# The queries of a windowed-attention kernel kept in the column order of their transposes

## The chip, the cores and the metric

The kernel runs on one core of a Trainium2 chip. The metric is the device time of one launch in microseconds. TensorE does matmuls and transposes, VectorE (DVE) and ScalarE (ACT) element-wise work, GpSimd (POOL) casts and small copies, and SyncE (SP) issues nearly all DMAs. SBUF is the on-chip memory, 128 partitions wide; matmuls write to PSUM.

## The reference

Attention over 4 batches, 8 heads, 768 positions of 64 numbers, and then a feed-forward layer over the 3072 tokens:

```
scores = scale * q @ k.T
keep   = is_global | is_local            # is_global: key < 8; is_local: 0 <= query - key < 96
bias   = -slopes[h] * dist               # dist: query - key, or 96 for a far global key
a      = softmax(where(keep, scores + bias, -1e9))
x      = (a @ v) as tokens x 512
out    = max(x @ w1, x @ w2, x @ w3) @ w_out     # 512 -> 768 -> 512
```

The inputs and the output are float32; the kernel's matmuls take bfloat16.

## The kernel before, in words

The tokens are cut into 24 tiles T of 128, six for each batch (NT = 6). A query tile needs its own keys and those of the tile before it (ds = 0, 1); the 8 global keys are copied over the first keys of each tile's transposed k. Scores are kept transposed, keys on the partitions and queries on the columns, so that exp(scores) can be the weights of the matmul with v. The bias is either multiplied in after the exponential (as exp(bias), VectorE, L319 and L321) or, for some tiles of batch 0, added ahead of it by a matmul with the identity (L289), for which the eight `bias` rows of L308 are made, one for each head.

All work is in one hand-written list, SCHEDULE (L25): each word is a unit, its tile and choices, and each engine meets its instructions in that order. Letters that matter here: `l` loads a pair of tiles of q or k (one part is 256 tokens; L148), `c` casts it (L180), `x` transposes it and copies the result to SBUF (`u_x`, L233), `S` makes the scores and the exponential of one tile and one half g of the heads (`u_S`, L282), `M` multiplies by the mask, `A` multiplies with v (L323), `T` transposes the result (L356), `F` and `O` are the two feed-forward matmuls (L376, L406), and `B` makes a bias row (`u_B`, L305), on ScalarE (0) or VectorE (1). The last number of `x` says which PSUM pool is used and which engine copies (odd: VectorE, even: ScalarE).

Tiles 0 to 11 (batches 0 and 1) come by `l`, `c`, `x`. Six q parts, and the last three k parts, are loaded with 8 neighbouring tokens on one partition (ET = 8, so that DMA descriptors are long): the row of partition (i, j) holds tokens 8i to 8i+7 of head j (and, by z, of head 4+j). So the eight transposes e = 0 to 7 (L255) give columns in the order (e, i, j), and the copy of L257 restores the order of the tokens for each head pair j: it reads PSUM with a step of 128 bf16 in its innermost run, and writes contiguous rows. The first three k parts have two neighbouring tokens on a partition and go by L250, one half copied by ScalarE and the other by VectorE. Tiles 12 to 23 come by other units (`L`, `C`, `X`), in token order.

In `u_S` one tile and one g have 8 score matmuls (4 for the first tile of a batch): weights are 64 rows by 128 keys, and the moving operand is 128 columns of q for the head pair jp. The halves z = 0 and 1 take partitions 0 to 63 and 64 to 127. They write `sp`, a PSUM tile of two banks with one buffer for each g; L302 is one exponential over all of it, 1024 columns (512 for the first tile of a batch), written as bfloat16 to `P`.

Of the kernel before, what the change touches and what calls it, by code (L numbers as in the profile page):

```python
# [14 lines left out]
AF = mybir.ActivationFunctionType  # L15
# [47 lines left out]
def kernel(  # L63
# [13 lines left out]
    nc = tc.nc  # L77
# [5 lines left out]
    NT = S // 128  # L83
    NTT = B * NT
    NP = H // 2
# [3 lines left out]
    scale = 1.0 / math.sqrt(D)  # L89
    slopes = [2.0 ** (-8.0 * (h + 1) / H) for h in range(H)]  # L90
    sizes = [4, 2, 2, 4, 4, 4, 4]

    ET = 8
# [30 lines left out]
    rbase = persist.tile([128, 3, 128], FP32, name="rbase")  # L124

    wmask = persist.tile([128, 2, 4, 3, 128], BF16, name="wmask")
    bias = persist.tile([128, 2, 2, 2, 3, 128], BF16, name="bias")
# [7 lines left out]
    raw, rawv, qb, qkT, Pt, xb = {}, {}, {}, {}, {}, {}  # L135
# [9 lines left out]
    def short_rows(n, s):  # L145
        return s == 1 and n < 3
# [31 lines left out]
    copies = (nc.scalar.copy, nc.vector.tensor_copy, nc.gpsimd.tensor_copy)  # L178
# [28 lines left out]
    def batch_T(b):  # L207
        if b not in qkT:
            qkT[b] = qkT_pool.tile([128, 2, NP, S], BF16, name="qkT", tag="qkT")
        return qkT[b]  # L210

    def qT(T, a):
        b, t = divmod(T, NT)
        return qkT[b][:, a, :, 128 * t:128 * t + 128]

    def put_kg(T, how):

        b, t = divmod(T, NT)
        kT = qT(T, 1)
        if t == 0:  # L220
            copies[how](kg8[b % 2], kT[:, :, 0:NG])
        elif t < NT - 1:
            copies[how](kT[:, :, 0:NG], kg8[b % 2])
# [9 lines left out]
    def u_x(n, s, how):  # L233
        b, t0 = divmod(2 * n, NT)
        dst = batch_T(b)[:, s, :, t0 * 128:(t0 + 2) * 128]
        if short_rows(n, s):
            dst = dst.rearrange("c j (i e) -> c j i e", e=2)
            if how == 4:
                halves = [(0, 2, psT, "tp", nc.scalar.copy), (2, 4, psH, "h", nc.vector.tensor_copy)]
            else:  # L240
                pool, tag = (psH, "h") if how in (2, 3) else (psT, "tp")
                halves = [(0, 4, pool, tag, copies[how % 2])]
            tps = [pool.tile([128, 2, hi - lo, 128], BF16, name="tpp", tag=tag) for lo, hi, pool, tag, copy in halves]
            for (lo, hi, pool, tag, copy), tp in zip(halves, tps):
                for e in range(2):
                    for j in range(lo, hi):
                        nc.tensor.transpose(tp[:, e, j - lo], qb["p", n, s][:, e, j].rearrange("p z d -> p (z d)"),
                                            identb)
            for (lo, hi, pool, tag, copy), tp in zip(halves, tps):
                copy(dst[:, lo:hi], tp.rearrange("c e j i -> c j i e"))  # L250
            return
        pool, tag = (psH, "h") if how in (2, 3) else (psT, "tp")
        tp = pool.tile([128, ET, 128 // NP, NP], BF16, name="tpp", tag=tag)
        for e in range(ET):
            nc.tensor.transpose(tp[:, e].rearrange("c i j -> c (i j)"),  # L255
                                qb["p", n, s][:, e].rearrange("p z d -> p (z d)"), identb)
        copies[how % 2](dst.rearrange("c j (i e) -> c j i e", e=ET), tp.rearrange("c e i j -> c j i e"))  # L257

    def u_X(T, how):
        pt = batch_T(T // NT)  # L260
# [21 lines left out]
    def u_S(T, g, how):  # L282
        b, t = divmod(T, NT)
        sp = psS.tile([128, 2, 2, 2, 128], FP32, name="sp", tag=f"sp{g}")
        n = 2 if t else 1
        if how:

            for hh in range(2):
                nc.tensor.matmul(sp[:, hh, :, 0:n], identb,  # L289
                                 bias[:, g, hh, :, 0:2] if t else bias[:, g, hh, :, 2:3],  # L290
                                 start=True, stop=False, skip_group_check=True)
        for ds in range(2 if t else 1):
            for i in range(2):
                jp = 2 * g + i
                for z in range(2):
                    hsl = slice(64 * z, 64 * z + 64)
                    nc.tensor.matmul(sp[:, z, i, ds], qT(T - ds, 1)[hsl, jp], qT(T, 0)[hsl, jp],  # L297
                                     start=not how, stop=True, skip_group_check=True)
        P = p_pool.tile([128, 4, 2, 128], BF16, name="P", tag="P")
        Pt[T, g] = P  # L300
        masked[T, g] = how
        nc.scalar.activation(P[:, :, 0:n], sp.rearrange("p a b d n -> p (a b) d n")[:, :, 0:n],  # L302
                             AF.Exp, bias=0.0, scale=scale)

    def u_B(h, how):  # L305
        z, g, i = h // 4, h % 4 // 2, h % 2
        mul = (nc.scalar.mul, nc.vector.tensor_scalar_mul, nc.gpsimd.tensor_scalar_mul)[how]
        mul(bias[:, g, z, i], rbase, -slopes[h] / scale)  # L308

    def u_K(h):  # L310
        z, g, i = h // 4, h % 4 // 2, h % 2
# [149 lines left out]
    with tc.manual_schedule():  # L461
        load_part(0, 0)
        load_part(0, 1)

        BIGD = 60000.0
        nc.gpsimd.iota(rbase[:, 0:2], base=0, pattern=[[128, 2], [1, 128]], channel_multiplier=-1,
                       allow_small_or_imprecise_dtypes=True)
        nc.vector.memset(tiny, 0.0)
        nc.scalar.activation(tiny, tiny, AF.Exp, bias=0.0, scale=1.0)
        nc.gpsimd.affine_select(rbase[:, 0:2], rbase[:, 0:2], base=(NL - 1),  # L470
                                pattern=[[-128, 2], [-1, 128]], channel_multiplier=1,
                                compare_op=ALU.is_ge, fill=BIGD)
        nc.vector.memset(zeros, 0.0)  # L473
        nc.gpsimd.affine_select(rbase[:, 0, :], rbase[:, 0, :], base=0,
                                pattern=[[1, 128]], channel_multiplier=-1,
                                compare_op=ALU.is_ge, fill=BIGD)
        nc.vector.memset(rbase[0:NG, 1, :], float(NL))
        nc.vector.tensor_copy(rbase[:, 2, :], rbase[:, 0, :])
        nc.vector.tensor_scalar_min(rbase[0:NG, 2, :], rbase[0:NG, 2, :], float(NL))
        make_identity(nc, identb)  # L480
        for tvar in va_ring + va_first:
            nc.vector.memset(heads(tvar)[:, :, 64:65], 1.0)

        units = {"l": load_part, "v": load_v, "c": cast_part, "x": u_x, "L": load, "w": load_w, "o": load_wo, "C": cast, "X": u_X, "S": u_S, "M": u_M,
                 "A": u_A, "G": put_kg, "V": put_vg, "T": u_XT, "F": u_F1, "W": cast_w,
                 "K": u_K, "B": u_B, "Q": cast_wo, "O": u_F2, "E": u_E, "D": u_D}
        for u in SCHEDULE.split():
            units[u[0]](*(int(n) for n in u[1:].split(".") if n))
# [33 lines left out]
```

## Time and profile before

| | us |
|---|---|
| median of 3 runs | 179.06 (178.82 to 180.25) |
| the profiled execution | 176.64 |
| its span, first to last instruction | 174.7 |
| TensorE busy | 168.3 (96%) |
| VectorE busy | 122.6 (70%) |
| ScalarE busy | 103.9 (59%) |
| GpSimd busy | 28.5 (16%) |
| granted TensorE clock | 1.000 |

The profile is a record of one execution. Its groups give, for each line, engine and shape, the count, the busy time and the mean duration, and then the engine's idle time ahead of these instructions with what ended it. The chain that ended last is followed back from the last instruction: at each step to what released it, or to the instruction before it on its engine. Matmuls are pipelined: one takes about 216 ns from start to end here, while the next starts much earlier, so their cost is read from groups that follow each other in the chain. TensorE's weight loads have their own row (PEld) and overlap with matmuls.

### The profile page before, as it was taken

How to read it: one execution, taken by the hardware profiler on the slowest of the kernel's cores; microseconds unless marked ns; L12 is line 12 of the kernel's file. 1: busy time of each engine (PE TensorE's matmuls, PEld its weight loads, DVE VectorE, ACT ScalarE, POOL GpSimd, SP SyncE). 2: the span in 40 equal slices, each digit the busy share in tenths (PEclk: the TensorE clock that was granted, in tenths of full speed). 3: DMA queues.
4: the chain of work that ended last, by engine and by line, in shares of the span. 5: the costliest groups of instructions: out<-in, count | busy, mean ns of one | idle time of the engine just before them, and what ended most of it. 6: DMA issues, size and time to landing. Idle time of an engine off the chain costs nothing.

```text
span 174.7 us, 3961 instructions
## 1 busy us (share of the span) xinstructions
PE 168.3 (96%) x1517; PEld 95.2 (54%) x1540; DVE 122.6 (70%) x254; ACT 103.9 (59%) x157; POOL 28.5 (16%) x58
## 2 busy tenths in 40 slices
PE   7879799999999999999999999999999999999996
PEld 2445555558866777854554454454544554444444
DVE  5478669897979799777888736799267993233720
ACT  7779769848999776776723665814857301342022
POOL 3245620100032521001041010203100300000000
DMA  4999999999999998999999899996965433401006
GB/s 134 323 283 284 327 341 342 383 387 385 239 228 211 283 248 160 158 264 236 196 188 231 119 298 254 204 195 120 249 158 155 89 94 90 180 0 60 6 3 237
DMA packets 82611, 36.44 MB, mean 209 GB/s; under 512 B 70048, under 2 KB 75040, under 8 KB 82592
## 3 DMA queue, kind: packets, MB, share of 16 engines
q1 hardware_dynamic: 82448, 36.12, 87.0%
q8 instruction: 12, 0.20, 0.5%
q10 hardware_dynamic: 144, 0.07, 0.1%
q14 instruction: 7, 0.06, 0.1%
HBM read 25.17 MB, written 6.29 MB: 180 GB/s over the span
## 4 chain that ended last, share of the span: by engine, by line
PE 90%; DMA 3%; SPq 2%; DVE 1%; issue 1%; ACT 1%; POOL 0%; DVEq 0%; POOLq 0%
PE h L382 54%; PE po L397 18%; PE sp L297 7%; DMA rawp<-in_q_dram 3%; PE op L336 3%; PE op L339 2%; PE tpp L255 2%; SPq L159 2%; PE oph L336 1%; PE wp L459 1%; PE sp L289 1%; PE xtp L370 1%; SPq L155 1%; ACT P L302 1%; DVE xT L371 1%
## 5 line engine op out<-in xcount | busy, mean ns | idle before, releaser
L382 PE MATMUL h<-xT,w 128*128 128x512 bf16 (+1 forms) x488 | 99.4, 348 | 1.1 <-issue 0.2
L382 PEld LDWEIGHTS <-w 128*128 128x128 bf16 x504 | 46.9, 98 | 40.0 <-issue 0.2
L302 ACT ACTIVATE P<-sp 128x1024 bf16<-128x1024 f32 (+1 forms) x48 | 43.6, 952 | 17.1 <-PE sp L297 16.9
L389 DVE TENSOR_TENSOR h<-h,h 128x512 bf16<-128x512 bf16 (+1 forms) x42 | 25.5, 608 | 15.9 <-PE h L382 13.0
L397 PE MATMUL po<-wo,ht 128*128 128x512 bf16 (+2 forms) x150 | 33.0, 362 | 0.3
L387 ACT CAST h<-h 128x512 bf16<-128x512 f32 (+1 forms) x42 | 21.8, 534 | 16.0 <-PE h L382 15.8
L391 DVE TENSOR_TENSOR ht<-h,h 128x512 bf16<-128x512 bf16 (+1 forms) x42 | 25.1, 606 | 4.5 <-PE h L382 3.2
L319 DVE TENSOR_TENSOR P<-P,wmask 128x1024 bf16<-128x1024 bf16 x35 | 24.5, 713 | 4.2 <-ACT P L302 4.2
L403 ACT COPY ost<-po 128x512 f32<-128x512 f32 (+2 forms) x17 | 9.4, 556 | 24.2 <-PE po L397 24.1
L397 PEld LDWEIGHTS <-ht 128*128 128x128 bf16 x156 | 14.3, 98 | 14.9
L297 PEld LDWEIGHTS <-qkT 64*128 64x128 bf16 x352 | 10.0, 94 | 10.0 <-issue 7.0
L297 PE MATMUL sp<-qkT 64*128 64x128 bf16 x352 | 14.7, 218 | 0.7 <-DVE qkT L257 0.3
L353 DVE TENSOR_TENSOR xb<-op,rz 128x512 bf16<-128x512 f32 x19 | 13.1, 691 | 0.7
L336 PEld LDWEIGHTS <-P 128*128 128x128 bf16 x192 | 12.2, 97 | 2.3 <-issue 0.3
L403 DVE COPY ost<-po 128x512 f32<-128x512 f32 (+1 forms) x9 | 5.8, 644 | 9.6 <-PE po L397 9.5
L339 PEld LDWEIGHTS <-P 128*128 128x128 bf16 x160 | 10.4, 97 | 1.2
L336 PE MATMUL op<-va,P 128*128 128x65 bf16 x136 | 10.5, 193 | 0.0
L195 POOL CAST va<-rawv 128x512 bf16<-128x512 f32 x11 | 6.8, 618 | 16.0 <-DMA rawv<-in_v_dram 15.9
L203 POOL CAST qkb<-raw 128x512 bf16<-128x512 f32 x8 | 6.2, 783 | 18.5 <-DMA raw<-in_k_dram 18.5
L339 PE MATMUL op<-va,P 128*128 128x65 bf16 x112 | 8.7, 193 | 0.2 <-POOL va L228 0.2
L352 DVE RECIPROCAL rz<-op 128x8 f32<-128x8 f32 x19 | 3.8, 202 | 6.5 <-PE op L339 4.5
L459 PE MATMUL wp<-zeros 128*128 128x512 bf16 x19 | 7.1, 539 | 1.3 <-DVE zeros L473 1.2
(72 smaller groups left out, 122.8 us busy)
## 6 DMA issues: line engine op xcount, KB each, us to landing
rawv<-in_v_dram SPq DMA_DIRECT2D x24, 256.0 KB, 5.0
out_dram<-ost SPq DMA_DIRECT2D x23, 256.0 KB, 2.8
rawp<-in_q_dram SPq DMA_DIRECT2D x12, 256.0 KB, 5.9
wst<-in_moe_w_dram SPq DMA_DIRECT2D x3, 1024.0 KB, 10.1
raw<-in_q_dram SPq DMA_DIRECT2D x12, 256.0 KB, 4.6
raw<-in_k_dram SPq DMA_DIRECT2D x12, 256.0 KB, 4.7
rawp<-in_k_dram SPq DMA_DIRECT2D x3, 512.0 KB, 5.8
wst<-in_moe_w_dram SPq DMA_DIRECT2D x3, 512.0 KB, 7.1
```

What stands on the lines that cost most here:

```text
L297: nc.tensor.matmul(sp[:, z, i, ds], qT(T - ds, 1)[hsl, jp], qT(T, 0)[hsl, jp], start=not how, stop=True, skip_group_check=True)
L302: nc.scalar.activation(P[:, :, 0:n], sp.rearrange("p a b d n -> p (a b) d n")[:, :, 0:n], AF.Exp, bias=0.0, scale=scale)
L319: nc.vector.tensor_mul(P, P, wmask[:, g, :, 0:2])
L336: nc.tensor.matmul(o, P[:, i, 0], heads(va[T])[:, h], start=True, stop=(t == 0), skip_group_check=True)
L339: nc.tensor.matmul(o, P[:, i, 1], heads(va[T - 1])[:, h], start=False, stop=True, skip_group_check=True)
L353: nc.vector.tensor_tensor(out=x.rearrange("p (g h) d -> p g h d", g=2), in0=o4[:, :, :, 0:64], in1=rz[:, :, :, None].to_broadcast([128, 2, ...
L382: nc.tensor.matmul(ps, w123[f // 2][:, dm, j, (f % 2) * 128:(f % 2) * 128 + 128], xT[c][:, dm], start=(dm == 0), stop=(dm == 3))
L387: nc.scalar.copy(h01, ps)
L389: nc.vector.tensor_max(h01s[c, f], h01s[c, f], ps)
L391: nc.vector.tensor_max(ht[c][:, f], h01s[c, f], ps)
L397: nc.tensor.matmul(po, ht[c][:, f, tt * 128:(tt + 1) * 128], wo[:, f, cols], start=(f == 0), stop=(f == NF - 1))
L403: copy(ost, po)
```

## The change

The q parts are copied from PSUM as they are, contiguous, 1024 columns in the order (e, i, j) for each pair of tiles. The score matmuls of tiles 0 to 11 read their 128 columns out of it: eight runs (e) of 16 columns (i) with a step of 4 bf16. The scores of these tiles then have their query columns in the order (e, i); the exponential reads PSUM with a step of 16 fp32 in its innermost run and writes `P` in token order. The bias rows, which are added to those scores, are written in the order (e, i) as well, with a step of 16 bf16. The k parts, the masks that are multiplied in, and tiles 12 to 23 are as they were. SCHEDULE is not changed: every engine has the same instructions in the same order.

```diff
+    def q_cols(T):
+        b, t = divmod(T, NT)
+        q4 = qkT[b][:, 0].rearrange("c j s -> c (j s)").rearrange("c (n e i j) -> c n e i j", n=NT // 2, e=ET, j=NP)
+        lo = 128 // ET * (t % 2)
+        return q4[:, t // 2, :, lo:lo + 128 // ET]
+
+    def mixed(T):
+        return T < 2 * NT
...
-        copies[how % 2](dst.rearrange("c j (i e) -> c j i e", e=ET), tp.rearrange("c e i j -> c j i e"))
+        if s == 0:
+            copies[how % 2](batch_T(b)[:, 0].rearrange("c j s -> c (j s)")[:, n % 3 * 1024:n % 3 * 1024 + 1024],
+                            tp.rearrange("c e i j -> c (e i j)"))
+        else:
+            copies[how % 2](dst.rearrange("c j (i e) -> c j i e", e=ET), tp.rearrange("c e i j -> c j i e"))
...
-                    nc.tensor.matmul(sp[:, z, i, ds], qT(T - ds, 1)[hsl, jp], qT(T, 0)[hsl, jp],
+                    o = sp[:, z, i, ds]
+                    if mixed(T):
+                        o, cols = o.rearrange("p (e i) -> p e i", e=ET), q_cols(T)[hsl, :, :, jp]
+                    else:
+                        cols = qT(T, 0)[hsl, jp]
+                    nc.tensor.matmul(o, qT(T - ds, 1)[hsl, jp], cols,
                                      start=not how, stop=True, skip_group_check=True)
...
-        nc.scalar.activation(P[:, :, 0:n], sp.rearrange("p a b d n -> p (a b) d n")[:, :, 0:n],
-                             AF.Exp, bias=0.0, scale=scale)
+        src = sp.rearrange("p a b d n -> p (a b) d n")[:, :, 0:n]
+        dst = P[:, :, 0:n]
+        if mixed(T):
+            if n == 2:
+                dst, src = dst.rearrange("p a d n -> p (a d) n"), src.rearrange("p a d n -> p (a d) n")
+            else:
+                dst, src = dst[:, :, 0], src[:, :, 0]
+            dst = dst.rearrange("p a (i e) -> p a i e", e=ET)
+            src = src.rearrange("p a (e i) -> p a i e", e=ET)
+        nc.scalar.activation(dst, src, AF.Exp, bias=0.0, scale=scale)
...
-        mul(bias[:, g, z, i], rbase, -slopes[h] / scale)
+        mul(bias[:, g, z, i].rearrange("p d (e i) -> p d i e", e=ET), rbase.rearrange("p d (i e) -> p d i e", e=ET),
+            -slopes[h] / scale)
```

More of the change, by code (lines that the diff above doesn't have):

```diff
@@ L286, in u_S @@
         if how:
+            assert mixed(T)
             for hh in range(2):
```

## The prediction

> **What bounds the kernel now.** I read the page's first two parts for the load, the chain of waits for what sets the end, the busy time by stretches for where each engine has room, and then the groups by shape for prices. Engines by share, then busy time by stretch:
>
> ```profile
> PE 168.3 (96%) x1517; PEld 95.2 (54%) x1540; DVE 122.6 (70%) x254; ACT 103.9 (59%) x157; POOL 28.5 (16%) x58
> ```
> ```profile
> 0.00:20.50 20.50, 16.89 (x192) 9.61 (x193) 13.94 (x42) 15.72 (x26) 9.13 (x23) 1.00 1.01 265
> 20.50:40.00 19.50, 19.20 (x164) 10.72 (x167) 15.75 (x27) 14.42 (x20) 2.63 (x4) 1.00 1.08 364
> 40.00:66.00 26.00, 25.79 (x324) 19.34 (x327) 22.29 (x56) 22.80 (x35) 6.45 (x11) 1.00 1.09 264
> ```
>
> The columns of a stretch are its length, then busy time of PE, PEld, DVE, ACT, POOL, the granted clock, the DMA share and GB/s. From 20.5 us on TensorE is busy over 98% of each of these stretches at clock 1.00, so whatever is added to TensorE there is added to the time. Before 20.5 it waits inside a chain, read in order of time (start, length, what):
>
> ```profile
> 4.80 5.17 DMA rawp<-in_q_dram
> 10.01 0.04 issue
> 10.06 0.70 DVE qkp L189
> 10.76 0.05 issue
> 10.81 0.62 PE tpp L255 x8
> 11.43 0.24 PE tpp L247 x4
> 11.69 0.59 ACT qkT L250
> 12.28 1.01 ACT P L302 x2
> 13.28 0.04 issue
> 13.33 0.59 PE sp L289 x2
> 13.92 0.33 PE sp L297 x8
> ...
> 15.27 0.33 PE sp L297 x8
> ...
> 16.42 0.33 PE sp L297 x8
> ...
> 24.59 0.55 PE sp L297 x16
> ```
>
> The reader should see three things. The chain starts from the second q load, which lands at 10.01. The q copy of L257 on VectorE is not in it. The score matmuls of L297 are, in the start and after it; 16 take 0.55 us and 8 take 0.33, so eight more cost 0.22: 27.5 ns each, 55 ns for the pair z=0, 1 that runs at once on two halves of the rows. A stream of 24 matmuls of 512 columns takes 5.18 us in the same chain (0.42 ns a column), so 128 columns need 54 ns. A pair goes at the streaming rate, and nothing hides a slower one.
>
> The prices of reads with a step, against contiguous ones:
>
> ```profile
> L257 ACT COPY qkT<-tpp 128x1024 bf16<-128x1024 bf16 x6 | 6.0, 1024 | 1.2 <-PE tpp L255 1.1
> L257 DVE COPY qkT<-tpp 128x1024 bf16<-128x1024 bf16 x3 | 3.7, 1220 | 0.7 <-PE tpp L255 0.7
> L250 DVE COPY qkT<-tpp 128x512 bf16<-128x512 bf16 x3 | 2.0, 682 | 0.0
> L371 DVE COPY xT<-xtp 128x512 bf16<-128x512 bf16 x6 | 2.3, 416 | 0.0
> L250 ACT COPY qkT<-tpp 128x512 bf16<-128x512 bf16 x3 | 1.8, 586 | 1.9 <-PE tpp L247 1.9
> ```
>
> **The change part by part.** Instructions keep their number and order on every engine, and no DMA or queue position moves; only durations can.
>
> *Six q copies become contiguous.* Two are on VectorE (parts 0 and 1). With a step, 512 more elements cost 1220-682 = 538 ns, 1.05 ns each; contiguous, 512 cost 416, of which about 150 is fixed (682-538 = 144), so 0.52 each. A contiguous 1024 is thus about 0.68 us: each saves 0.54, 1.07 in all. Neither is on the chain. The first releases a score matmul that waited 0.35 us for it at 8.73, but ScalarE then ends those exponentials earlier only to wait for the part that lands at 10.01. The second ends at 12.69, while its reader at 12.84 waits for ScalarE's exponential. I take 0, and -1.07 as the bound. Four are on ScalarE: L250 with a step takes 586 ns, the contiguous 512 of L371 585. They gain 0.
>
> *Eight bias rows are written with a step of 16 bf16.* No row shows a stepped write. The five on VectorE take 347 ns for 384 elements, about 0.52 each. At 1.05 they take 0.55; at twice that, 0.95. Four of them start at 2.65 and at worst end near 6.45; VectorE then idles until 6.58 (2.8 us of idle before it now). The fifth stands ahead of the first q copy: at most +0.60 against that copy's -0.54, inside the 0.42 us that VectorE idles before 10.06. The three on ScalarE (0.51 each) have 0.82 us of idle behind them. I take 0. Were that cover gone, the fifth's 0.60 would fall on the cast at 10.06, and so on the chain.
>
> *24 exponentials read PSUM with a step of 16 fp32.* Nearest rows: ScalarE's copies of L257 and L250 read PSUM with steps of 128 and 256 bf16 at (1024-586)/512 = 0.86 ns an element, and the contiguous exponentials at (1024-596)/512 = 0.84. [...] I take 0; these rows are 2-byte reads, so the upper bound is twice the element time, +0.86 us for 1024. Ten of them also wait on an exponential six back, long done; a row of such a wait on ScalarE is 17 ns, at most 0.2 us there, where the stretch 20.5 to 66 has 45.5-37.2 = 8.3 us free.
>
> [...]
>
> *176 score matmuls read q with a step of 4 bf16 in runs of 16.* This decides. All of before's matmuls read contiguous columns, so the price must be bounded. Below: 54 ns a matmul as now, so 0. A gain is excluded, since a contiguous read already streams at 0.42 ns a column. Above: stepped reads in the rows run at 0.84 to 0.86 ns an element on ScalarE and 1.05 on VectorE. VectorE, the only reader shown to go faster than that on contiguous data (0.52), loses half its rate by the step. TensorE reads at 0.42, twice as fast as any stepped read here. I take the faster of the two rows, 0.85: 128 columns take 108 ns, +54 a pair; at 1.05, 134 ns, +80. After 20.5 us tiles 4 to 11 have 120 of these matmuls, 60 pairs: 60 x 54 = 3.2 us, all on TensorE's path. In the start the chain passes the three groups of 8 shown (12 pairs) and about a pair of tile 0's: 13 x 54 = 0.7. Who waits: the exponentials, 24 times, and behind each group the in-order matmuls of the feed-forward.
>
> [...]
>
> **Sum.** 0 + 0 + 0 + 3.2 + 0.7 = +3.9 us. The profiled execution took 176.6 (span 174.7 and 1.9 around it), so 180.5; against the median of the runs, 179.06, which lies 2.4 above that execution, 183.0.
>
> **Rivals.** *B, the step is free to TensorE.* [...] For it: ScalarE's rows, where a step costs nothing. Against it: VectorE's halved rate. Then only the q copies remain: 179.1, down to 178.0 if all of the 1.07 us reached the end, and it decides if a pair stays under about 75 ns (73 pairs x 20 = 1.5 us). This is the side where the kernel is not slower. [...]
>
> *C, the exponentials slow.* At 4 bytes a step may halve ScalarE. Six exponentials (five full ones' worth) feed one another from 12.17 to 17.88 with about 0.4 us of idle: 5 x 0.86 - 0.4 = +3.9. After 20.5, 15 full ones' worth are 12.9 us against 8.3 free: +4.6. In all 187.6. Against it: the stepped ScalarE rows. It matters from about +0.2 us each on. [...]
>
> *D, faster by over 1%.* It would need 1.8 us out of copies that save 1.07 off the chain; no row offers it.
>
> **How the numbers follow.** A (stepped read costs TensorE) 0.50, B 0.32, C 0.13, D 0.05. About 1% (1.8 us) is what a measurement of this kernel can tell from no change. The forecast is A's 183.0. A's own range is 181.0 (27 ns more a pair, half of what I took: 73 x 27 = 2.0) to 184.9 (73 x 80 = 5.8). The whole range takes in B down to 178.0 and A up to 185.0, and leaves out C and D, 0.18. Faster 0.05; same 0.34 (B, and a little of A under 25 ns a pair); slower 0.61 (the rest of A, and C).
>
> **What would show it.** In the profile after: groups of 16 score matmuls of tiles 4 to 11 at about 0.98 us in the chain, not 0.55, while tiles 12 to 23 keep 0.55; the first feed-forward matmul near 21.2, not 20.53; VectorE's q copies near 0.68; full exponentials of tiles 0 to 11 at 1.02; bias rows between 0.35 and 0.95. It is wrong if those groups keep 0.55 us (B), if the exponentials of tiles 0 to 11 exceed about 1.2 us (C), or if VectorE's cast at 10.06 moves back because of the bias rows.

## The result, and the profile after

The changed kernel takes 185.4 us (184.5 to 185.9, 4 runs) against 178.94 for the kernel before (177.1 to 180.3): 1.039 times as long, 95% interval 1.030 to 1.049. Medians, here and below, are of all runs, while ratios and intervals are of the means of fast runs alone, because some executions of a kernel fall into a slower state. The change is slower, as forecast, but by 6.5 us (7.0 between the means behind the ratio) where 3.9 were worked out, and 0.4 us above the upper end of the range. The profiled execution took 184.54 us, its span is 182.7, 8.0 more than before.

The groups by shape, first before and then after (mean ns behind the bar and the comma):

```profile
L302 ACT ACTIVATE P<-sp 128x1024 bf16<-128x1024 f32 x40 | 39.2, 1024 | 14.9 <-PE sp L297 14.6
L308 DVE TENSOR_SCALAR bias<-rbase 128x384 bf16<-128x384 f32 x5 | 1.5, 347 | 0.0
L308 ACT ACTIVATE bias<-rbase 128x384 bf16<-128x384 f32 x3 | 1.5, 512 | 0.5 <-DVE rbase L479 0.5
```

```profile
L330 ACT ACTIVATE P<-sp 128x1024 bf16<-128x1024 f32 x40 | 39.3, 1023 | 18.5 <-PE sp L316 18.3
L335 DVE TENSOR_SCALAR bias<-rbase 128x384 bf16<-128x384 f32 x5 | 8.5, 1917 | 0.0
L335 ACT ACTIVATE bias<-rbase 128x384 bf16<-128x384 f32 x3 | 5.6, 1861 | 0.5 <-DVE rbase L507 0.5
L268 ACT COPY qkT<-tpp 128x1024 bf16<-128x1024 bf16 x4 | 4.1, 1014 | 1.2 <-PE tpp L265 1.1
L268 DVE COPY qkT<-tpp 128x1024 bf16<-128x1024 bf16 x2 | 1.6, 782 | 1.7 <-PE tpp L265 1.7
```

The exponentials kept their 1023 ns with the step of 16 fp32, and the q copies did nearly what was foreseen: on VectorE 0.69 and 0.87 us (the mean is 0.78) for 1.22, where 0.68 was expected, and no change on ScalarE. The bias rows did not: 1.92 us on VectorE for 0.35, 1.86 on ScalarE for 0.51.

The chain that ended last, after, in order of time (start, length, what):

```profile
4.12 5.26 DVE bias L335 x3
9.38 0.52 DVE qkp L189
9.90 1.69 DVE bias L335
...
11.63 1.01 PE sp L303 x2
12.64 0.55 PE sp L316 x8
...
19.51 0.54 PE sp L316 x8
...
25.15 0.38 PE h L410
...
29.21 1.00 PE sp L316 x16
...
80.93 0.55 PE sp L316 x16
```

Two things are new. The start no longer begins with a load: VectorE's bias rows stand in its place, and the first feed-forward matmul (`PE h`, 25.15 us) starts 4.62 us later than before:

```profile
20.53 0.38 PE h L382
```

And a group of 16 score matmuls takes 1.00 us for tiles 4 to 11 (29.21 is tile 4), while those of tiles 12 on keep 0.55 (80.93). From the first feed-forward matmul to the end it is 182.7 - 25.15 = 157.55 us, before 174.7 - 20.53 = 154.17: 3.38 more. So 4.6 of the 8.0 us are lost in the start and 3.4 behind it.

In order of time, the start shows who waits (start, length, engine, line). First VectorE's cast of the first k load before, then the same place after:

```profile
6.58 0.69 DVE L189 CAST qkp<-rawp 128x1024 bf16<-128x1024 f32 x1 [2.77 <-DMA rawp<-in_k_dram]
```

```profile
9.01 0.89 DVE L189 CAST qkp<-rawp 128x1024 bf16<-128x1024 f32 x1
...
9.95 0.62 PE L257 MATMUL tpp<-identb,qkp 128*128 128x128 bf16 x8 [3.55 <-DVE qkp L189]
10.48 0.60 ACT L260 COPY qkT<-tpp 128x512 bf16<-128x512 bf16 x1
```

The cast of k, which began when its load landed at 6.58, now begins at 9.01 behind four bias rows. TensorE stands for 3.55 us waiting for it, and then its granted clock is lower for a while, 0.66 in the mean of 12 to 16 us (third figure from the end):

```profile
8.00:12.00 4.00, 0.99 (x9) 0.61 (x10) 4.00 (x4) 3.07 (x5) 1.09 (x1) 0.91 1.11 260
12.00:16.00 4.00, 4.00 (x41) 1.89 (x40) 2.18 (x6) 2.29 (x3) 1.33 (x3) 0.66 1.08 270
```

Two bias matmuls of L303 take 1.01 us at 11.63, where the clock is 0.50; before they took 0.59 at 13.33, at clock 1.00. The cast of the second q load moves back from 10.06 to 12.89, which the prediction had named as a sign of being wrong.

### The profile page after: what moved, and what is told of

The parts are those of the page before. It is cut to its first block, busy times and chain, and to the rows that moved or that the text cites. A ratio compares the mean times of both kernels' runs of the same rounds, so it can differ in the third digit from the quotient of the medians.

```text
span 182.7 us, 3971 instructions
## 1 busy us (share of the span) xinstructions
PE 172.8 (95%) x1517; PEld 97.5 (53%) x1540; DVE 129.9 (71%) x254; ACT 107.9 (59%) x157; POOL 27.1 (15%) x58
## 4 chain that ended last, share of the span: by engine, by line
PE 90%; DVE 6%; issue 2%; ACT 1%; POOL 1%; POOLq 0%
PE h L410 52%; PE po L425 17%; PE sp L316 9%; DVE bias L335 4%; PE op L364 3%; PE op L367 2%; PE sp L303 2%; PE tpp L265 2%; PE oph L364 1%; PE wp L487 1%; ACT P L330 1%; PE xtp L398 1%; DVE xT L399 1%; PE oph L367 0%; DVE xb L381 0%
## 5 line engine op out<-in xcount | busy, mean ns | idle before, releaser
L316 PE MATMUL sp<-qkT 64*128 64x128 bf16 x352 | 19.5, 251 | 0.3
L316 PEld LDWEIGHTS <-qkT 64*128 64x128 bf16 x352 | 13.0, 100 | 10.4 <-issue 7.7
L195 POOL CAST va<-rawv 128x512 bf16<-128x512 f32 x11 | 7.4, 676 | 7.9 <-ACT qkb L205 3.2
L335 DVE TENSOR_SCALAR bias<-rbase 128x384 bf16<-128x384 f32 x5 | 8.5, 1917 | 0.0
L238 POOL COPY va<-vaf 8x260 int32<-8x260 int32 x9 | 3.5, 393 | 31.1 <-PE op L367 8.8
```

What stands on the lines that cost most here:

```text
L316: nc.tensor.matmul(o, qT(T - ds, 1)[hsl, jp], cols, start=not how, stop=True, skip_group_check=True)
L335: mul(bias[:, g, z, i].rearrange("p d (e i) -> p d i e", e=ET), rbase.rearrange("p d (i e) -> p d i e", e=ET), -slopes[h] / scale)
```

## The experiments

Theory T says that there are two separate costs, the stepped bias writes (start) and the stepped q reads (every score matmul of tiles 0 to 11). Its rivals are S, that the reads and the low clock make the late start; H, that the reads' eight runs cost and not their step; W and D, that the exponentials or the copies move the end.

**Bias rows contiguous, reads stepped.** A second position table is made in the order (e, i).

```diff
-        mul(bias[:, g, z, i].rearrange("p d (e i) -> p d i e", e=ET), rbase.rearrange("p d (i e) -> p d i e", e=ET),
-            -slopes[h] / scale)
+        mul(bias[:, g, z, i], rbp, -slopes[h] / scale)
```

> The changed kernel, with a second position table whose columns stand in the order (e, i) from the start, so that the eight bias rows are written contiguously; the score matmuls still read q with a step of 4. Theory T (two separate costs: the stepped bias writes delay the start, the stepped reads slow every score matmul): bias rows back to 0.35 us on VectorE and 0.51 on ScalarE, the first feed-forward matmul near 21.2 us (20.53 plus 0.7 for about 13 slower pairs) and not 25.15, groups of 16 score matmuls still 1.00 us; about 183.0 us. Rival S (the start is late because of the slower score matmuls and TensorE's lower clock there, and the bias rows have room): the first feed-forward matmul stays past 24 us; about 185.

Measured: 182.07 us against 179.01, ratio 1.019 (1.009 to 1.029); rows back to 0.34 and 0.51 us, groups of 16 at 1.00. In its profiled execution the first k load landed late (cast at 8.46 us), so that one's first feed-forward matmul, at 24.43, does not tell T from S. The next experiment and the last but one do.

**Reads contiguous, bias rows stepped.**

```diff
-                        o, cols = o.rearrange("p (e i) -> p e i", e=ET), q_cols(T)[hsl, :, :, jp]
+                        q0 = 1024 * (t // 2) + 512 * (t % 2) + 128 * jp
+                        cols = qkT[b][:, 0].rearrange("c j s -> c (j s)")[hsl, q0:q0 + 128]
```

> The changed kernel, but the score matmuls of tiles 0 to 11 read 128 contiguous columns of the same q block, which are not the right tokens: the order of the queries is left out, the amount of work is not. The bias rows are still written with the step of 16. Theory T: groups of 16 score matmuls back to 0.55 us, bias rows still 1.8 to 2.0 us, the first feed-forward matmul near 24.4 us; 185.4 - 3.4 - 0.7 = about 181.3 us. Rival S: the first feed-forward matmul near 21; about 179.

Measured: 181.3 us against 179.01, ratio 1.017 (1.010 to 1.025). Groups are back to 0.55 us, and the start is late without any stepped read:

```profile
4.11 5.36 DVE bias L336 x3
...
12.75 0.54 PE sp L317 x8
...
18.11 0.33 PE sp L317 x8
...
24.73 0.38 PE h L411
...
28.79 0.55 PE sp L317 x16
```

The first feed-forward matmul is at 24.73, after the change at 25.15. So S falls: the bias rows make the start late without any slower read. The lower clock is here too: TensorE waits 3.6 us for the cast of k, and the clock is 0.56 from 8 to 12 us and 0.58 from 12 to 16. The two ratios multiply to 1.019 x 1.017 = 1.037; the whole change measured 1.039. A contiguous group of 8 takes 0.54 us at 12.75 and 0.33 at 18.11; the granted clock is 0.58 in the 4 us from 12 on and 1.00 in the 4 us from 16 on. After the change a stepped group takes 0.55 at 12.64 and 0.54 at 19.51, with the clock at 0.50 and 1.00 during these two groups. So TensorE's clock does not set the pace of the stepped read.

**Both contiguous.** The two edits above together; the order of the queries is left out.

> The changed kernel with both costs taken out: bias rows written contiguously from a table already in the order (e, i), and the score matmuls of tiles 0 to 11 reading 128 contiguous columns of their q block (the order of the queries is left out there). The contiguous q copies and the exponential's step of 16 fp32 stay. Theory T (bias writes and stepped q reads are all of the loss, and the copies bring nothing): within 1% of the kernel before, near 179 us, groups of 16 at 0.55 us. Rival W (the exponentials' steps or their added waits cost too): over 181. Rival D (the VectorE time saved by the copies does reach the end): under 178.

Measured: 177.29 us (10 runs) against 177.55, ratio 0.999 (0.996 to 1.002).

```profile
10.80 0.70 DVE qkp L190
...
21.27 0.38 PE h L411
...
25.33 0.55 PE sp L318 x16
```

The exponentials' stepped reads, their ten added waits and the contiguous q copies are all still there, and together they move nothing. Nor does a gain hide a loss in the start: from the cast of the second q load to the first feed-forward matmul it is 21.27 - 10.80 = 10.47 us here and 20.53 - 10.06 = 10.47 before. W and D fall: the copies' 1.07 us of VectorE time is worth nothing where it lies, as the prediction had it.

**Head-major partitions**, so that a score matmul reads eight contiguous runs of 16.

```diff
-                nc.sync.dma_start(out=r[:, z], in_=src[4 * z:4 * z + 4].rearrange("h (i e) d -> i h (e d)", e=ET))
+                nc.sync.dma_start(out=r[:, z], in_=src[4 * z:4 * z + 4].rearrange("h (i e) d -> h i (e d)", e=ET))
```

> As the kernel with contiguous bias rows, and the loads put the four heads of a part on the partitions one after the other (j, i) instead of interleaved (i, j), so that q stands in the order (e, j, i) and a score matmul reads eight contiguous runs of 16 columns, 256 bytes apart. The q copies stay contiguous and the exponential still restores the order. Theory T (it is the step inside a run that costs): groups of 16 back to 0.55 us, first feed-forward matmul near 20.5, about 179 us, within 1% of the kernel before, and not faster, since the q copies on VectorE are not on the chain. Rival H (it is the eight runs with their hops that cost): groups stay at 1.00 us and the time near 183.

Measured: 218.7 us, ratio 1.226. The time missed what T and H expected, for a reason outside both: the groups of 16 in the chain are at 0.55 us, but the loads came late. The same order of loads put alone into the kernel before settles it:

> The kernel before with only the loads' order on the partitions changed: the four heads of a part one after the other instead of interleaved, and the copies after the transposes adapted. Theory L (the loads in that order are what made the kernel with head-major partitions slow): about 215 us, DMA share well under 0.9 in the first 60 us. Rival (something else in that kernel): near 178.

Measured: 219.2 us in one run, 178.08 for the kernel before. A stretch of it (the last two figures are DMA share and GB/s):

```profile
10.00:20.00 10.00, 4.22 (x36) 2.42 (x36) 2.87 (x5) 2.52 (x3) 2.29 (x3) 0.67 0.48 121
```

and of the kernel before:

```profile
10.00:20.00 10.00, 8.18 (x140) 5.58 (x141) 8.29 (x21) 8.51 (x12) 4.90 (x11) 1.00 1.18 291
```

The loads arrive at 121 GB/s where it was 291, and the DMA share is 0.48 where it was 1.18. That the order of the loads does it is shown; by what, is not.

**A price list**: another read pattern for each tile, another write step for each bias row.

> A price list and not the reference's output: the score matmuls of each tile read q in another pattern, out of place, and the bias rows are written in other orders. Groups of 16 score matmuls by tile: 4 as in the change, 5 one run with a step of 4, 7 a step of 2, 8 a step of 8, 9 a step of 16 in two runs, 10 eight contiguous runs of 16, 11 a step of 3. [...] Theory T: any step of 2 or more costs about the same 1.00 us (the read takes one column where it took two), runs cost nothing. Rival G (the cost grows with the bytes stepped): 2 between 0.55 and 1.00, 8 and 16 above 1.00. Bias rows on VectorE in their order: steps of 2, 4, 8 and 32 elements, then one that reads with a step of 8 fp32 and writes contiguously; on ScalarE one contiguous, one with the stepped read, one with a step of 4. [...] No time is expected of the whole.

Measured: 180.87 us in one run. The groups of 16 in its chain, for tiles 4, 5, 7, 8, 9, 10, 11:

```profile
24.84 1.00 PE sp L339 x16
...
27.67 1.02 PE sp L339 x16
...
44.53 0.57 PE sp L339 x16
...
50.45 1.91 PE sp L339 x16
...
56.66 1.95 PE sp L339 x16
...
60.91 0.55 PE sp L339 x16
...
66.41 0.79 PE sp L339 x16
```

One run with a step of 4 costs what eight runs do (1.02, 1.00), and eight contiguous runs cost nothing (0.55). So H falls: the step is the cost. It is not one price for any step, as T had it; it grows from step 2 (0.57) over 3 (0.79) and 4 (1.00) to 8 (1.91) and then stops (16: 1.95). The number of 16-byte stretches that the read touches accounts for all of these; the prices below are estimates from these groups. A contiguous group of 16 is 8 pairs of 55 ns and about 0.11 us for the last to end. Step 3 touches 48 stretches for 128 columns: (0.79 - 0.11)/8/48 = 1.77 ns each. Step 4, 64: 1.74. Step 8, 128: 1.76. Step 16, 128: 1.80. Step 2 touches 32, which need 56 ns, hardly more than the 54 that the columns need; contiguous columns touch 16, which would need 28.

The bias rows of the same run: the stepped writes (first fence line VectorE, second ScalarE), then the rows that read with a step of 8 fp32 and write contiguously:

```profile
L365 DVE TENSOR_SCALAR bias<-rbase x4: 631/1461/2085, 2.6 to 5.5; 128x384 bf16<-128x384 f32 x4
L365 ACT ACTIVATE bias<-rbase x1: 1057/1057/1057, 5.6 to 5.6; 128x384 bf16<-128x384 f32 x1
```
```profile
L360 ACT ACTIVATE bias<-rbase x1: 891/891/891, 4.0 to 4.0; 128x384 bf16<-128x384 f32 x1
L360 DVE TENSOR_SCALAR bias<-rbase x1: 822/822/822, 8.0 to 8.0; 128x384 bf16<-128x384 f32 x1
```

VectorE's four stepped writes, in their order, take 0.63 us (step 2, 96 stretches), 0.99 (step 4, 192), 1.93 (step 8, 384) and 2.09 (step 32, 384). With some 0.15 us fixed (an estimate from the contiguous rows: 347 ns less 384 x 0.52 on VectorE, and 0.19 from 512 less 384 x 0.84 on ScalarE) that is 5.0, 4.4, 4.6 and 5.0 ns a stretch; the change's step of 16 gives (1.98 - 0.15)/384 = 4.8, and ScalarE's step of 4 (1.06 - 0.19)/192 = 4.5. A read with a step of 32 bytes, where every element lies in another stretch, costs (0.82 - 0.15)/384 = 1.74 ns an element on VectorE and 1.82 on ScalarE, nearly the same as a stretch on TensorE. Other steps of a read were not run on these two engines.

**One engine's rows at a time**, on the kernel with both contiguous.

> As the kernel with both costs out, but VectorE's five bias rows are written with the step of 16 (1.8 to 2.0 us each) and ScalarE's three are contiguous. Theory T (VectorE's rows stand ahead of the casts and the q copy that the start's chain needs, so they carry the delay): near the 181.3 us of the kernel in which only the reads were contiguous, the first cast of k on VectorE past 8.5 us. Rival (ScalarE's rows carry it): near 179.

> As the kernel with both costs out, but ScalarE's three bias rows are written with the step of 16 (about 1.86 us each) and VectorE's five are contiguous. Theory T: ScalarE ends its rows and masks near 10.5 us instead of 7, and its first k copy moves back by up to 2.5 us where the loads land early and by less where they land late; 179 to 180.5 us, less than with VectorE's rows. Rival (ScalarE's rows carry the delay): near 181.3.

Measured: VectorE's rows 183.08 us, ratio 1.032 (1.028 to 1.036); ScalarE's 181.47, ratio 1.024 (1.020 to 1.027). Both are more than was expected. The second position table makes the stepped rows start 1.4 us later (4.0 instead of 2.65) than in the change, so these sizes cannot be added to those above. What the two runs show is that, with this later start, either engine's rows alone make the start late: the first feed-forward matmul is at 26.16 and 24.84 us, with both contiguous at 21.27. The chain with ScalarE's rows:

```profile
4.08 1.86 ACT bias L338
5.95 0.72 ACT wmask L345 x2
6.67 1.75 ACT bias L338
8.42 0.72 ACT wmask L345 x2
9.14 1.72 ACT bias L338
10.86 1.14 ACT wmask L345 x3
11.99 0.48 ACT qkT L261
...
24.84 0.38 PE h L415
```

In the change the two delays lie beside each other, and the longer sets the start: ScalarE is free for its first k copy at 10.48 us, while VectorE's fifth row ends near 11.6 and the chain goes through it.

**The bias rows permuted on the read side**, in the change.

```diff
-        mul(bias[:, g, z, i].rearrange("p d (e i) -> p d i e", e=ET), rbase.rearrange("p d (i e) -> p d i e", e=ET),
+        mul(bias[:, g, z, i].rearrange("p d (e i) -> p d e i", e=ET), rbase.rearrange("p d (i e) -> p d e i", e=ET),
             -slopes[h] / scale)
```

> The changed kernel, but the bias rows are permuted on the other side: they read the position table with a step of 8 fp32 (32 bytes) and write contiguously. By the price list such a row takes 0.82 us on VectorE and 0.89 on ScalarE, inside the 0.95 that the prediction had as the upper bound. Theory T (the prediction's cover was right and only the price of the stepped write was not): VectorE's four rows end before 6 us, the cast of k starts when its load lands, the first feed-forward matmul within 1 us of 20.53 to 21.09, groups of 16 at 1.00 us; the loss is the score matmuls' alone, about 4 us over the kernel before, with a ratio near 1.022. Rival (any slower bias row moves the start): first feed-forward matmul past 23 us.

Measured: 181.68 us against 178.08, ratio 1.021 (1.009 to 1.032). Its rows, and its chain:

```profile
L335 DVE TENSOR_SCALAR bias<-rbase x5: 836/843/861, 2.6 to 8.1; 128x384 bf16<-128x384 f32 x5
L335 ACT ACTIVATE bias<-rbase x3: 883/884/897, 2.7 to 6.0; 128x384 bf16<-128x384 f32 x3
```
```profile
10.78 0.70 DVE qkp L189
...
22.05 0.38 PE h L410
...
26.11 1.00 PE sp L316 x16
```

Rows of 0.84 us, more than twice as long as before, are covered, and the start waits for loads again. The rival falls, and S with it: stepped score matmuls alone put the first feed-forward matmul at 22.05, not past 24. From there to the end it is 179.6 - 22.05 = 157.55 us, as in the change.

**The kernel before once more.**

> The kernel before once more, for a second profile of its start. If the landing of the first k load moves from execution to execution, as the spread of the runs (177.0 to 180.5) and the profile of the kernel with contiguous bias rows (cast of k at 8.46 us against 6.58) suggest, this profile has the first feed-forward matmul at another time than 20.53 us, with the rest of the span as long as before (154.2 us from that matmul on). If not, 20.5 again.

Measured: 177.25 us in one run. The first feed-forward matmul is at 21.09, and the cast of k at 7.32 instead of 6.58. From that matmul to the end it is 175.3 - 21.09 = 154.21 us, as before (154.17). So a start is to be compared only with one whose loads landed alike: 0.6 us of the change's 4.62 can be this. Among the kernels above, the one with both contiguous and the one with rows permuted on the read side start the cast of k alike, at 7.50 and 7.49. By these the 4.62 us are 25.15 - 22.05 = 3.10 for the bias rows, 22.05 - 21.27 = 0.78 for the score matmuls, and 21.27 - 20.53 = 0.74 for loads that landed later.

No version that beats the kernel before came out of this: with both costs gone, and the order of the queries left out for it, the ratio is 0.999.

## Why the prediction was right and wrong

- *The chain, and that whatever is added to TensorE is added to the time:* right behind the start, where 60 pairs that take 56 ns more added 3.38 us.
- *Stepped score matmuls, 3.2 + 0.7 us:* right in size. The pair's 108 ns, taken from a ScalarE row, measured 111. The start's 0.7 measured 22.05 - 21.27 = 0.78 (rows permuted on the read side against both contiguous, loads landing within 0.02 us of each other). That the number fitted is luck: the rows from which the 0.85 ns came were ScalarE's own pace on PSUM, while the price is 1.74 to 1.80 ns for each 16-byte stretch of SBUF and has nothing to do with them. At a step of 3 or 8, where a group of 16 took 0.79 and 1.91 us, the same working would have been off.
- *Rival B, the step is free to TensorE:* it falls. With a step of 4 a read takes two columns from each 16-byte stretch, and a group of 16 takes 1.00 us for 0.55. At 0.42 ns a column it would take four columns to fill the 1.76 ns of a stretch (an estimate from these groups), and at a step of 2, which has four, the group took 0.57.
- *Exponentials at 0:* right, 1023 ns with the step (fp32, 64 bytes apart) and 1024 before. Rival C falls: its +0.86 us for a full exponential was the author's estimate, and no run shows any of it.
- *q copies at 0 for the end:* right; 0.999 with all else removed.
- *Eight bias rows at 0:* this step failed. "At 1.05 they take 0.55; at twice that, 0.95" was given as an upper bound, and nothing in the trace made it one: no row showed a stepped write, and the nearest rows were reads from PSUM. The rows took 1.77 to 2.02 us. The cover was worked out right (rows of 0.84 us are hidden, as the read-side run shows), and the text named what lies behind it, but priced the lost cover at the fifth row's 0.60. In fact four rows of nearly 2 us ran past the k load and held the cast until 9.01; TensorE waited 3.55 us, and its granted clock was 0.50 from 11.63 to 13.19 us. The kernel with this cost alone took 1.017 times as long, 3.1 us between the means behind that ratio, and its first feed-forward matmul came 3.5 to 4.2 us later (24.73 against 21.27 and 20.53).
- *The range:* its upper end took in 5.8 us for the score matmuls and nothing for the bias rows, though their price was the other unknown. With a bound that allowed for what was not shown, 185.4 would have been inside.

## What to carry to other kernels

An upper bound must come from a row of the same kind: a stepped write to SBUF is not bounded by a stepped read of PSUM. Where no such row exists, ask how long the operation may take before its cover is gone, and give that case a price and a chance, however small the operation looks. And a permutation moved off a copy that was not on the chain gains nothing, and it can be paid at every place that meets the new order: here nothing in the exponentials, 56 ns in each pair of score matmuls and 1.4 to 1.6 us in each bias row. If it must be undone on VectorE or ScalarE, do it on the side that reads (0.84 us for a VectorE row and 0.89 for a ScalarE row, 1.92 and 1.86 on the side that writes), and best where ScalarE reads PSUM, which cost nothing (1023 ns for 1024).

## What the runs showed of the hardware

- A moving operand that TensorE read from SBUF with a step of 3, 4, 8 or 16 bf16 cost 1.74 to 1.80 ns for each 16-byte stretch it touched (groups of 16 matmuls at 0.79, 1.00, 1.91 and 1.95 us). A step of 2 was almost hidden (0.57 us a group for 0.55).
- A read of fp32 from SBUF with a step of 32 bytes cost VectorE 1.74 and ScalarE 1.82 ns an element (rows of 384 at 0.82 and 0.89 us), where every element lies in another such stretch.
- A write of bf16 to SBUF with a step cost 4.1 to 5.0 ns for each such stretch, on VectorE (steps 2, 4, 8, 16 and 32) and ScalarE (4 and 16): with a step of 16 a row of 384 elements took VectorE 1.92 us for 0.35 and ScalarE 1.86 for 0.51.
- Reads of PSUM with a step cost ScalarE nothing in the two cases run: 1023 ns for 1024 at 4-byte elements 64 bytes apart, and 586 ns with a step of 512 bytes and 585 without one at 2-byte elements.
- A stepped read of the moving operand ran at the same rate at a granted TensorE clock of 0.50 and 1.00 (0.55 and 0.54 us for 8 matmuls), where a contiguous one took 0.54 us in a stretch of mean clock 0.58 and 0.33 in one of 1.00.
- Loads of 2 KB rows that walk one head after the other instead of four in turn moved 121 GB/s for 291 from 10 to 20 us, with a DMA share of 0.48 for 1.18.
